# Moving the routing of a mixture-of-depths kernel: gate scores from V, comparisons on GpSimd, half stores on SP

## The chip, the cores and the metric

The kernel runs on one core of one Trainium2 chip. The metric is the device time of one execution in microseconds (us), lower is better; it is given as the median of the runs. "Span" is the time from the first to the last instruction in the profiled execution. The engines are called PE (TensorE, matmul), PEld (its weight loads), DVE or VectorE, ACT or ScalarE, POOL or GpSimd, and SP (SyncE, here a queue for DMAs).

## The reference

Two layers follow each other. The first is attention in chunks of 32 tokens: each chunk sees 16 tokens to its left, 8 to its right and 8 memory tokens of its head. The second is a mixture of depths: of the 768 tokens of a batch, the 128 with the highest gate score pass through a two-layer expert, and the result, times the sigmoid of the score, is added to the token.

```python
# attention: q, k, v are (4, 8, 768, 64); mem_k, mem_v are (4, 8, 8, 64)
for c in range(24):
    k_full = concat(mem_k, k[:, :, max(0, 32*c - 16) : min(768, 32*c + 40)])
    v_full = concat(mem_v, v[...same tokens...])
    a = softmax(q_c @ k_full.T / 8)
    out[:, :, 32*c : 32*c + 32] = a @ v_full
# mixture of depths: x is (4, 768, 512), the heads side by side
scores = x @ w_gate
for b in range(4):
    top = the 128 tokens with the largest scores[b]
    h = max(x[b, top] @ w1, 0)              # 512 -> 1024
    out[b, top] += sigmoid(scores[b, top])[:, None] * (h @ w2)
```

## The kernel before

**Pairs.** The work is cut into 16 pairs of heads (`n`), four to a batch. The main loop over `n` is written so that three pairs are in work at once. In iteration `n` stand, in this order: scores of pair n+1, first half (`scores`, PE matmuls, then three exponentials on ACT, L271); transposes of q for pair n+2 (`tr_q`); values of pair n, first half (`values`, L292); transposes of k for pair n+2 (`tr_k`); scores of n+1, second half; V of n+1 turned back (`back_v`, L250 and L251); values of n, second half; transposes of v for n+2 (`tr_v`). `values` multiplies the exponentials with 64 columns of V and a column of ones, so that column 64 of the result is the sum of the softmax; VectorE takes its reciprocal (L295) and writes x (L296). The 8 memory columns of k and v are copied into place on GpSimd (`mem_cols`, L224): those of kw(n+2) after VectorE's copy (L232), those of vw(n+3) earlier in the iteration.

**Routing.** For a finished batch the kernel runs these steps, each named `m_...`:

- `m_dot`: six multiply-and-accumulate instructions on VectorE (L335), the gate scores `scr`
- `m_row`: PE transposes the scores so that each partition sees all 768 of them, ACT copies them to `brow`
- `m_gate_exp`, `m_gate`: the sigmoid, an exponential on ACT and four small operations on VectorE (L361 to L365)
- `m_cmp`: six comparisons 128x768 of the row with each token's score (L373)
- `m_count`: 36 matmuls with a column of ones count them (L383), six per comparison
- `m_mask`, `m_slot`, `m_sel`: the chosen tokens, their places, and one-hot columns `sel`
- `m_fetch`: token numbers `idx` by six matmuls (`m_aux`, L438), then an indirect DMA on GpSimd's queue fetches the 128 rows from the stored output (L412)
- `m_rows`, `m_ffn1` (two halves, L453), `m_ffn2` (L462): the expert; then `y` on ACT and an indirect DMA that adds it to the output (L466)

**Order.** The order on each engine is the order of the program text. `moe_steps` gives each step of batch b a place, counted in eighths of a pair from the start of batch b+1; `hook(i)` in the loop emits what is due. Batches 0 and 1 have their comparisons at places 18, 19, 22, 23, 24 and 27 and their counts at 30 and 31; batch 2 has a denser list. Weights and later q, k and v are loaded by DMAs of GpSimd's queue at the end of some iterations (`load_w` in pairs 0, 2, 4 and 6, `load_unit` in pairs 1, 3, 5 and 7).

**The last batch.** Batch 3 has no later loop to hide in. Its dots over the first two pairs stand in iteration 15; after the loop come the store of x, the dots over the last two pairs, and the remaining steps by hand, with the expert of batch 2 among them. It doesn't fetch its rows: `m_gather` (L428) picks them by matmuls with `sel` from a half-precision copy `x16`. `fill` is a matmul with zeros that computes nothing.

**Buffers.** The PSUM pools `pxx` (values), `pvv`, `ptt` and `pmm` (routing) have one buffer each, `pss` has two. Batch 3 takes `pss` for its routing.

Of the kernel before, what the change touches and what calls it, by code (L numbers as in the profile page):

```python
# [17 lines left out]
def _dap(x, offset, dims):  # L18
    return bass.AP(tensor=x.tensor, offset=offset, ap=[list(d) for d in dims])
# [7 lines left out]
def kernel(  # L27
# [13 lines left out]
    nc = tc.nc  # L41
# [11 lines left out]
    NPR = B * NP  # L53
    SLOTS = 4

    cst = ctx.enter_context(tc.tile_pool(name="cst", bufs=1))
# [93 lines left out]
    for i in range(SLOTS):  # L150
        vcs.append(cst.tile([128, NG, 2, 66], F16, tag=f"vc{i}", name=f"vc{i}"))
        kws.append(cst.tile([128, NG, 128], F16, tag=f"kw{i}", name=f"kw{i}"))
        vws.append(cst.tile([128, NG, 128], F16, tag=f"vw{i}", name=f"vw{i}"))
        nc.vector.tensor_copy(out=vcs[i][:, :, :, 64], in_=ones8[:, :].unsqueeze(2).to_broadcast([128, NG, 2]))
# [19 lines left out]
    onec = cst.tile([128, 1], F16, tag="onec")  # L174
    zero6 = cst.tile([128, NB], F16, tag="zero6")
    auxs = [cst.tile([128, NB, 3], F16, tag=f"aux{i}", name=f"aux{i}") for i in range(2)]
    w1_sb = cst.tile([128, 4, F], F16, tag="w1")
    w2_sb = cst.tile([128, 8, Dm], F16, tag="w2")

    def late_constants():  # L180
        nc.vector.tensor_copy(out=ident, in_=ident16)
        nc.vector.memset(ones6, 1.0)
        nc.vector.memset(onec, 1.0)
        nc.vector.memset(zero6, 0.0)
        nc.gpsimd.iota(iota1, pattern=[[1, cap]], base=1, channel_multiplier=0, allow_small_or_imprecise_dtypes=True)
        nc.gpsimd.memset(ltri, 1.0)
        nc.gpsimd.affine_select(out=ltri, in_=ltri, pattern=[[1, 128]], compare_op=ALU.is_gt, fill=0.0,
                                base=0, channel_multiplier=-1)
        for a in auxs:
            nc.gpsimd.iota(a[0:96, :, 0], pattern=[[96, NB]], base=0, channel_multiplier=1,  # L190
                           allow_small_or_imprecise_dtypes=True)
            nc.gpsimd.iota(a[96:128, :, 0], pattern=[[32, NB]], base=576, channel_multiplier=1,
                           allow_small_or_imprecise_dtypes=True)

    def load_w(i):
# [49 lines left out]
    def back_v(n):  # L245
# [5 lines left out]
        nc.vector.tensor_copy(out=vcs[n % SLOTS][:, :, :, 0:64], in_=p_v)  # L251

    GROUPS = ((0, 1, 2, 6), (3, 4, 5, 7))
    ess = {}
# [22 lines left out]
    def values(n, half, fills=0):  # L277
# [8 lines left out]
        fill_into(p_w, fills)  # L286
        p_x = p_w[:, 0:390].rearrange("p (i h c) -> p i h c", i=3, h=2)
        for r0, r1, gis in ((0, 96, (0, 1, 2)), (96, 128, (3, 3, 3))):
            for i, gi in enumerate(gis):
                q0, q1 = (0, 96) if gi < 3 else (32 * i, 32 * i + 32)  # L290
                for h in range(2):
                    nc.tensor.matmul(out=p_x[r0:r1, i, h, :], lhsT=es[:, h, gi, q0:q1],  # L292
                                     rhs=vc[:, GROUPS[half][gi], h, 0:65], start=True, stop=True)
        rd = att.tile([128, 3, 2, 1], FP, tag="rd", name="rd")
        nc.vector.reciprocal(out=rd, in_=p_x[:, :, :, 64:65])  # L295
        nc.vector.tensor_tensor(  # L296
            out=xs[b].rearrange("p g (n h d) -> p n g h d", n=NP, d=D)[:, pr, 3 * half:3 * half + 3],
            in0=p_x[:, :, :, 0:64], in1=rd.to_broadcast([128, 3, 2, D]), op=ALU.mult)

# [14 lines left out]

    def m_store(b):
        x = xs[b]

        eng = nc.gpsimd if b == LAST else nc.sync
        eng.dma_start(out=_dap(out, b * S * Dm, [[Dm, 96], [96 * Dm, NB], [1, Dm]]), in_=x[0:96, :, :])
        eng.dma_start(out=_dap(out, (b * S + 576) * Dm, [[Dm, 32], [32 * Dm, NB], [1, Dm]]), in_=x[96:128, :, :])  # L320

# [6 lines left out]

    def m_dot(b, bls, pr0=0, pr1=NP, dst=None):
        m, x = mods[b], xs[b]  # L330
        dst = m.scr if dst is None else dst
        for bl in bls:
            c0, c1 = 2 * D * pr0, 2 * D * pr1
            junk = mod.tile([128, Dm], FP, tag="junk", name="junk")
            nc.vector.scalar_tensor_tensor(out=junk[:, c0:c1], in0=x[:, bl, c0:c1], scalar=1.0, in1=wgb[:, c0:c1],  # L335
                                           op0=ALU.mult, op1=ALU.mult, accum_out=dst[:, bl:bl + 1])

# [3 lines left out]

    def m_row(b, lo, hi, eng=None):
        m = mods[b]
        p_b = m_bank(b, None)
        for bl in range(lo, hi):
            nc.tensor.transpose(out=p_b[:, 0, 128 * (bl - lo):128 * (bl - lo) + 128],
                                in_=m.scr[:, bl:bl + 1].to_broadcast([128, 128]), identity=ident)
        o, i = m.brow[:, 128 * lo:128 * hi], p_b[:, 0, 0:128 * (hi - lo)]
        if eng == "dve":
            nc.vector.tensor_copy(out=o, in_=i)  # L350
        else:
            nc.scalar.copy(out=o, in_=i)

# [12 lines left out]

    def m_cmp(b, bls):

        m = mods[b]
        if 0 in bls:  # L370
            m.gr = mod.tile([128, NB, S], F16, tag="gr", name="gr")
        for bl in bls:
            nc.vector.tensor_scalar(out=m.gr[:, bl, :], in0=m.brow, scalar1=m.scr[:, bl:bl + 1], scalar2=None,  # L373
                                    op0=ALU.is_lt)

# [47 lines left out]
    def m_gather(b):  # L423
        m = mods[b]
        p_e = m_bank(b, None)
        for dch in range(4):
            for bl in range(NB):
                nc.tensor.matmul(out=p_e[:, 0, 128 * dch:128 * dch + 128],  # L428
                                 lhsT=m.x16[:, bl, 128 * dch:128 * dch + 128],
                                 rhs=m.sel[:, bl, :], start=(bl == 0), stop=(bl == NB - 1))  # L430
        m.xeT = mod.tile([128, 4, 128], F16, tag="xeT", name="xeT")
        nc.scalar.copy(out=m.xeT.rearrange("p c t -> p (c t)"), in_=p_e[:, 0, :])

# [23 lines left out]

    def m_ffn2(b):
        m = mods[b]
        p_y = m_bank(b, None)  # L460
        for fch in range(8):
            nc.tensor.matmul(out=p_y[:, 0, :], lhsT=m.hT[:, fch, :], rhs=w2_sb[:, fch, :],  # L462
                             start=(fch == 0), stop=(fch == 7))
        y = mod.tile([128, Dm], FP, tag="y", name="y")
        nc.scalar.activation(out=y, in_=p_y[:, 0, :], func=AF.Copy, scale=m.gate[:, 0:1])  # L465
        nc.gpsimd.indirect_dma_start(out=outf[0:(b + 1) * S, :], out_offset=bass.IndirectOffsetOnAxis(ap=m.idx[:, :1], axis=0),  # L466
                                     in_=y[:, :], in_offset=None, compute_op=ALU.add)

    def moe_steps(b):
# [3 lines left out]
        def at(i, f, *a):  # L473
            st.setdefault(i, []).append(lambda: f(b, *a))
# [6 lines left out]
        if b == LAST - 1:  # L481
            p = dict(dots=(0, 1, 3, 4, 6, 7), row0=9, row1=11, gate=12, cmps=(13, 14, 15, 17, 18, 19),
                     counts=(21, 21, 21, 22, 22, 22), mask=22, slot=24, sel=24, fetch=24)
        for i in range(NB):
# [5 lines left out]
        for i in range(NB):  # L490
            at(p["cmps"][i], m_cmp, (i,))
        for i in range(NB):
# [18 lines left out]
    def hook(i):  # L511
        for f in places.get(i, ()):
            f()
# [22 lines left out]
    late_constants()  # L536
    scrA = mod.tile([128, NB], FP, tag="scrA", name="scrA")
    scrB = mod.tile([128, NB], FP, tag="scrB", name="scrB")
    for n in range(NPR):
        b, pr = divmod(n, NP)  # L540
# [4 lines left out]
        if n == 1:  # L545
            nc.sync.dma_start(out=wgb, in_=_dap(moe_w_gate, 0, [[0, 128], [1, Dm]]))
        if n == NPR - 2:
            m_alloc(LAST)
        scores(n + 1, 0)
        hook(i)  # L550
        if n == NPR - 1:
            m_dot(LAST, range(NB), 0, 2, scrA)
        if 3 <= n + 3 < NPR:
            mem_cols(vws[(n + 3) % SLOTS], memvT, n + 3)
        tr_q(n + 2)
        hook(i + 1)
        values(n, 0, nf)
        hook(i + 2)
# [5 lines left out]
        hook(i + 4)  # L564
        back_v(n + 1)
        hook(i + 5)
        values(n, 1, 1)
        hook(i + 6)
# [8 lines left out]

    b = LAST
    m_store(b)
    m_dot(b, range(NB), 2, 4, scrB)  # L580
    nc.vector.tensor_tensor(out=mods[b].scr, in0=scrA, in1=scrB, op=ALU.add)
    fill(8)
    m_rows(b - 1)
    m_row(b, 0, 4)
    m_gate_exp(b)
    m_row(b, 4, 6, "dve")
    m_ffn1(b - 1, 0)
    m_ffn1(b - 1, 1)
    m_cmp(b, range(NB))
    m_ffn2(b - 1)  # L590
    m_x16(b, 0, 6, 2, 4)
    m_count(b, range(NB))
    m_mask(b)
    m_slot(b)
    fill(3)
    m_sel(b)
# [41 lines left out]
```

## Time and profile before

| What | Value |
|---|---|
| Median of 3 runs | 141.28 us |
| Lowest and highest | 140.58 and 144.77 us |
| Profiled execution, its own time | 139.08 us |
| Its span | 137.4 us |
| Busy: PE, PEld | 111.7 us (81%), 83.0 us (60%) |
| Busy: DVE, ACT, POOL | 87.5 us (64%), 80.0 us (58%), 50.5 us (37%) |
| Mean granted clock of TensorE | 0.936 |
| Comparisons L373 on VectorE | 24, mean 0.62 us |
| Dots L335 on VectorE | 30, mean 0.58 us |

The profile tells of one execution. A line of a timeline has the start, the time taken, the engine, the line of the kernel, the operation, what it writes and reads with shape and type, a count where several were merged, and in brackets how long the engine had been idle and what ended that. The windows view has one row for each stretch of time: busy time of PE, PEld, DVE, ACT and POOL with the number of instructions, then the clock that TensorE was granted, the mean busy share of the DMA engines and the GB/s.

### The profile page before, as it was taken

To read this page: it belongs to the slowest core of one execution; us is meant where nothing else is said; L and a number is where in the kernel's file an instruction comes from. 1 tells how busy PE (TensorE), PEld (TensorE's weight loads), DVE (VectorE), ACT (ScalarE), POOL (GpSimd) and SP (SyncE) were. 2 spreads that over 40 slices of the span, in tenths; PEclk is the share of its full clock that TensorE was granted. 3 is DMA by queue.
4 is the path that set the end of the run, shared out by engine and by line. 5 is a ranking of instruction groups with operands and counts; after the bars stand their busy time and mean duration, and the time that the engine had idled before them with its cause. 6 is when DMAs were issued, how large, how long until landed. Compare 5 with 4: busy or idle time off the path is not lost.

```text
span 137.4 us, 4727 instructions
## 1 busy us (share of the span) xinstructions
PE 111.7 (81%) x2024; PEld 83.0 (60%) x2024; DVE 87.5 (64%) x280; ACT 80.0 (58%) x159; POOL 50.5 (37%) x84
## 2 busy tenths in 40 slices
PE   6997688977998978989997999897797897888500
PEld 2355376866777756867885858685656555458100
DVE  3444556574799399889738955997954896651000
ACT  4047958779779859565676947858748005153300
POOL 6996364352683634914200226121004140040130
PEclk9999999999999999995599999999999559999995
DMA  2999999999999999999991002973001439606050
GB/s 63 173 146 184 203 206 206 205 212 206 205 248 287 278 208 206 205 235 290 286 185 23 0 7 19 268 252 43 0 5 12 67 38 260 203 0 81 0 70 6
DMA packets 15397, 19.90 MB, mean 145 GB/s; under 512 B 848, under 2 KB 11536, under 8 KB 15376
## 3 DMA queue, kind: packets, MB, share of 16 engines
q0 software_dynamic: 12832, 14.62, 63.4%
q1 hardware_dynamic: 2544, 4.98, 11.0%
q8 instruction: 16, 0.26, 0.7%
q14 instruction: 5, 0.04, 0.1%
HBM read 24.25 MB, written 7.34 MB: 230 GB/s over the span
## 4 chain that ended last, share of the span: by engine, by line
PE 31%; DVE 15%; ACT 14%; issue 14%; DMA 14%; POOL 6%; POOLq 1%
ACT es L271 7%; DMA q<-in_q_dram 7%; PE p_w L292 7%; PE p_t L210 5%; PE p_v L250 4%; DMA xe<-out_dram,idx 3%; DMA out_dram<-y,idx 3%; DVE junk L335 3%; DVE x L296 3%; ACT qT L219 3%; PE p_w L116 3%; PE p_m L462 3%; PE p_m L453 2%; DVE gr L373 2%; PE p_m L383 2%
## 5 line engine op out<-in xcount | busy, mean ns | idle before, releaser
L271 ACT ACTIVATE es<-p_s,maskb 128x256 f16<-128x256 f32 x96 | 38.8, 485 | 3.2 <-PE p_s L266 3.1
L292 PEld LDWEIGHTS <-es 128*32 128x32 f16 (+1 forms) x384 | 22.1, 116 | 4.4 <-issue 0.7
L292 PE MATMUL p_w<-vc,es 128*32 128x65 f16 (+1 forms) x384 | 24.4, 208 | 0.0
L242 ACT COPY vw<-p_t 128x960 f16<-128x960 f16 x16 | 15.4, 962 | 14.5 <-PE p_t L210 14.5
L224 POOL COPY kw<-memkT 128x64 f16<-128x64 f16 x12 | 8.0, 666 | 36.4 <-DVE kw L232 36.4
L296 DVE TENSOR_TENSOR x<-p_w,rd 128x384 f32<-128x384 f32 x32 | 17.8, 558 | 1.1
L219 ACT COPY qT<-p_q 128x768 f16<-128x768 f16 x16 | 13.0, 813 | 7.4 <-PE p_q L210 7.4
L335 DVE SCALAR_TENSOR_TENSOR junk<-x,wgb 128x512 f32<-128x512 f32 (+1 forms) x30 | 16.2, 582 | 0.0
L466 POOL DMA_INDIRECT out_dram<-y,idx x4 | 6.5, 1635 | 24.7 <-ACT y L465 23.4
L295 DVE RECIPROCAL rd<-p_w 128x6 f32<-128x6 f32 x32 | 6.1, 191 | 12.5 <-PE p_w L292 12.1
L373 DVE TENSOR_SCALAR gr<-brow,scr 128x768 f16<-128x768 f32 x24 | 14.0, 623 | 0.1
L116 PE MATMUL p_f<-zeros 128*128 128x512 f16 x36 | 12.8, 496 | 1.3 <-DVE zeros L110 1.3
L250 PE MATMUL p_v<-ident,vw 128*128 128x128 f16 x128 | 10.2, 225 | 4.3 <-ACT qT L219 4.3
L251 DVE COPY vc<-p_v 128x1024 f16<-128x1024 f16 x16 | 11.0, 687 | 4.3 <-PE p_v L250 4.1
L232 DVE COPY kw<-p_t 128x1024 f16<-128x1024 f16 x16 | 10.9, 683 | 3.5 <-PE p_t L210 3.4
L266 PE MATMUL p_s<-qT,kw 64*128 64x96 f16 x256 | 11.3, 209 | 0.3 <-POOL kw L224 0.3
L250 PEld LDWEIGHTS <-vw 128*128 128x128 f16 x128 | 8.1, 100 | 5.6 <-issue 4.1
L116 PEld LDWEIGHTS <-zeros 128*128 128x128 f16 x60 | 5.9, 110 | 8.9 <-issue 4.6
L210 PE MATMUL p_q<-ident,q 96*64 96x96 f16 x256 | 8.8, 213 | 2.6 <-DMA q<-in_q_dram 2.5
L116 PE MATMUL p_w<-zeros 128*128 128x512 f16 x24 | 9.8, 410 | 1.0 <-DVE x L296 1.0
L210 PEld LDWEIGHTS <-q 96*64 96x64 f16 x256 | 6.7, 113 | 4.5 <-DMA q<-in_q_dram 2.7
L453 PEld LDWEIGHTS <-w_sb 128*128 128x128 f16 x128 | 7.6, 97 | 2.5 <-issue 1.6
(112 smaller groups left out, 165.0 us busy)
## 6 DMA issues: line engine op xcount, KB each, us to landing
out_dram<-x SPq DMA_DIRECT2D x3, 1152.0 KB, 11.5
k<-in_k_dram POOLq DMA_DIRECT2D x7, 384.0 KB, 13.2
q<-in_q_dram POOLq DMA_DIRECT2D x7, 384.0 KB, 13.7
v<-in_v_dram POOLq DMA_DIRECT2D x7, 384.0 KB, 14.6
w_sb<-in_moe_w_dram POOLq DMA_DIRECT2D x8, 256.0 KB, 13.4
out_dram<-x SPq DMA_DIRECT2D x3, 384.0 KB, 13.2
out_dram<-x POOLq DMA_DIRECT2D x1, 1152.0 KB, 6.8
k<-in_k_dram POOLq DMA_DIRECT2D x2, 192.0 KB, 4.8
```

Of the source, the lines that this page charges most:

```text
L116: nc.tensor.matmul(out=ap, lhsT=zeros[:, 0:128], rhs=zeros, start=True, stop=True)
L210: nc.tensor.transpose(out=dst[64 * h:64 * h + 64, j, :], in_=src[n][:, h, 64 * j:64 * j + 64], identity=ident16[0:96, 0:96])
L219: nc.scalar.copy(out=qT, in_=p_q.rearrange("p j t -> p t j"))
L242: nc.scalar.copy(out=vw.rearrange("p g (j t) -> p g j t", t=16)[:, :, :, 0:15], in_=_sap(p_t, 0, [[12, NG], [100, 8], [1, 15]]))
L250: nc.tensor.transpose(out=p_v[:, g, :, :], in_=vws[n % SLOTS][:, g, :], identity=ident16)
L251: nc.vector.tensor_copy(out=vcs[n % SLOTS][:, :, :, 0:64], in_=p_v)
L266: nc.tensor.matmul(out=p_s[:, h, 96 * gi:96 * gi + 96], lhsT=kw[o:o + 64, g, :], rhs=qf[o:o + 64, 96 * g:96 * g + 96], start=True, stop=True)
L271: nc.scalar.activation(out=es[:, :, :, 32 * c:32 * c + 32], in_=pv[:, :, :, 32 * c:32 * c + 32], func=AF.Exp, bias=maskb[:, c:c + 1], scal ...
L292: nc.tensor.matmul(out=p_x[r0:r1, i, h, :], lhsT=es[:, h, gi, q0:q1], rhs=vc[:, GROUPS[half][gi], h, 0:65], start=True, stop=True)
L296: nc.vector.tensor_tensor(out=xs[b].rearrange("p g (n h d) -> p n g h d", n=NP, d=D)[:, pr, 3 * half:3 * half + 3], in0=p_x[:, :, :, 0:64] ...
L335: nc.vector.scalar_tensor_tensor(out=junk[:, c0:c1], in0=x[:, bl, c0:c1], scalar=1.0, in1=wgb[:, c0:c1], op0=ALU.mult, op1=ALU.mult, accum ...
L373: nc.vector.tensor_scalar(out=m.gr[:, bl, :], in0=m.brow, scalar1=m.scr[:, bl:bl + 1], scalar2=None, op0=ALU.is_lt)
```

## The change

Four things are changed.

1. For pairs 14 and 15 (`WGN` is 14) V gets two more columns per head: V times the gate weights of that head, as a half-precision value and its remainder (`gate_columns` once, `gate_v` for each of the two pairs). `values` then yields the gate score's share in columns 65 and 66; `score` scales it by the reciprocal and adds it up. `values` returns the write of x and the score as two functions, so that the caller places them. The dots over the first two pairs of batch 3 move from iteration 15 into iteration 14.
2. `m_cmp` runs on GpSimd unless an engine is given. That holds for all comparisons of batches 0 and 1 and for the first four of batch 2. The last two of batch 2 and all of batch 3 stay on VectorE.
3. The last store goes out in two halves on SP (`m_store` with `lo` and `hi`), each after its half of x.
4. Batch 2 gets earlier places, so that its fetch is issued in iteration 14; the loop ends with iteration 14, and pair 15 is written out after it, with steps of batch 3 and the expert of batch 2 in turns. `m_ffn2` can be done in two halves. `m_gather` now goes over the token blocks outside and the four column blocks inside, after a matmul with zeros that opens the bank. The fills after the loop are gone.

```diff
-        vcs.append(cst.tile([128, NG, 2, 66], F16, tag=f"vc{i}", name=f"vc{i}"))
+        vcs.append(cst.tile([128, NG, 2, 68], F16, tag=f"vc{i}", name=f"vc{i}"))
...
+    def gate_columns():
+
+        nc.vector.memset(wgd, 0.0)
+        for h in range(2):
+            r = slice(64 * h, 64 * h + 64)
+            nc.vector.tensor_copy(out=wgd[r, :, h, 0], in_=wgT[r, :])
+            nc.vector.tensor_tensor(out=wgd[r, :, h, 1], in0=wgT[r, :], in1=wgd[r, :, h, 0], op=ALU.subtract)
...
+    def gate_v(n, p_g):
+
+        vc = vcs[n % SLOTS]
+        for g in range(NG):
+            nc.tensor.matmul(out=p_g[:, 4 * g:4 * g + 4], lhsT=vws[n % SLOTS][:, g, :],
+                             rhs=wgd[:, n - WGN, :, :].rearrange("p h c -> p (h c)"), start=True, stop=True)
+        gv = att.tile([128, NG, 2], FP, tag="gv", name="gv")
+        nc.vector.reduce_sum(out=gv, in_=p_g[:, 0:4 * NG].rearrange("p (g h c) -> p g h c", h=2, c=2),
+                             axis=mybir.AxisListType.X)
+        nc.vector.tensor_copy(out=vc[:, :, :, 65], in_=gv)
+        nc.vector.tensor_tensor(out=vc[:, :, :, 66], in0=gv, in1=vc[:, :, :, 65], op=ALU.subtract)
...
+        def score():
+
+            t = parts[n - WGN][half]
+            nc.vector.tensor_tensor(out=t[:, :, 0:4].rearrange("p i (h c) -> p i h c", c=2), in0=p_x[:, :, :, 65:67],
+                                    in1=rd.to_broadcast([128, 3, 2, 2]), op=ALU.mult)
+            o = mods[b].scr[:, 3 * half:3 * half + 3] if n == NPR - 1 else parts[1][half][:, :, 4]
+            nc.vector.reduce_sum(out=o, in_=t, axis=mybir.AxisListType.X)
...
-            nc.vector.tensor_scalar(out=m.gr[:, bl, :], in0=m.brow, scalar1=m.scr[:, bl:bl + 1], scalar2=None,
-                                    op0=ALU.is_lt)
+            (eng or nc.gpsimd).tensor_scalar(out=m.gr[:, bl, c0:c1], in0=m.brow[:, c0:c1],
+                                             scalar1=m.scr[:, bl:bl + 1], scalar2=None, op0=ALU.is_lt)
...
-            p = dict(dots=(0, 1, 3, 4, 6, 7), row0=9, row1=11, gate=12, cmps=(13, 14, 15, 17, 18, 19),
-                     counts=(21, 21, 21, 22, 22, 22), mask=22, slot=24, sel=24, fetch=24)
+            p = dict(dots=(0, 1, 2, 3, 4, 5), row0=7, row1=9, gate=11, cmps=(10, 10, 10, 10, 11, 13),
+                     counts=(16,) * NB, mask=16, slot=19, sel=20, fetch=22)
...
-            at(p["cmps"][i], m_cmp, (i,))
+            at(p["cmps"][i], m_cmp, (i,), nc.vector if b == LAST - 1 and i > 3 else None)
...
-    for n in range(NPR):
+    for n in range(NPR - 1):
...
+            nc.sync.dma_start(out=wgT, in_=_dap(moe_w_gate, 2 * D * (WGN % NP), [[1, 128], [2 * D, 2]]))
+        if n == 4:
+            gate_columns()
...
-        if n == NPR - 1:
-            m_dot(LAST, range(NB), 0, 2, scrA)
...
-        values(n, 0, nf)
+        vA = values(n, 0, nf)
+        vA[0]()
+        if n == NPR - 2:
+            m_dot(LAST, (0, 1, 2))
+            vA[1]()
...
+        if n == NPR - 2:
+            gate_v(n + 1, p_t.bitcast(FP).rearrange("p j t -> p (j t)")[:, 0:4 * NG])
+            m_dot(LAST, (3, 4, 5))
...
-    b = LAST
-    m_store(b)
-    m_dot(b, range(NB), 2, 4, scrB)
-    nc.vector.tensor_tensor(out=mods[b].scr, in0=scrA, in1=scrB, op=ALU.add)
-    fill(8)
+    b, n = LAST, NPR - 1
+    A, Bh = range(3), range(3, 6)
+    vA = values(n, 0)
+    vA[1]()
+    vB = values(n, 1)
+    m_row(b, 0, 3, pxx.tile([128, 512], FP, tag="px", name="p_r"))
+    vB[1]()
+    vA[0]()
+    m_store(b, 0, 3)
+    m_row(b, 3, 6, pvv.tile([128, 512], FP, tag="pv", name="p_r"))
+    m_gate_exp(b)
     m_rows(b - 1)
-    m_row(b, 0, 4)
-    m_gate_exp(b)
-    m_row(b, 4, 6, "dve")
+    m_x16(b, 0, 3, 2, 4)
+    m_cmp(b, A, nc.vector, 0, S // 2)
     m_ffn1(b - 1, 0)
+    m_cmp(b, A, nc.vector, S // 2, S)
     m_ffn1(b - 1, 1)
-    m_cmp(b, range(NB))
-    m_ffn2(b - 1)
-    m_x16(b, 0, 6, 2, 4)
-    m_count(b, range(NB))
+    m_cmp(b, Bh, nc.vector)
+    vB[0]()
+    m_x16(b, 3, 6, 2, 4)
+    m_store(b, 3, 6)
+    m_count(b, A)
+    m_ffn2(b - 1, 0, 4)
+    m_count(b, Bh)
     m_mask(b)
     m_slot(b)
-    fill(3)
+    m_ffn2(b - 1, 4, 8)
     m_sel(b)
     m_gate(b)
     m_gather(b)
```

## The prediction

> **What bounds the kernel now.** I read the 40 slices first, then the time of each pair of heads (from one reciprocal of a pair's second half, L295, to the next), then the timeline around the routing of each batch, and last the tail.
>
> No engine bounds the span (PE 81%, DVE 64% busy), so each stage has its own limit. In the windows view (columns PE, PEld, DVE, ACT, POOL busy, clock, DMA share, GB/s) pairs 6, 9, 12 and 14 read:
>
> ```profile
> 44.66:51.24 6.58, 5.32 (x124) 4.17 (x121) 4.28 (x14) 4.65 (x11) 3.05 (x6) 1.00 1.19 245
> ...
> 62.75:69.71 6.96, 6.96 (x106) 5.74 (x108) 5.41 (x14) 4.54 (x9) 2.70 (x4) 0.59 1.15 276
> ...
> 83.67:91.30 7.63, 6.90 (x168) 5.58 (x168) 6.74 (x26) 4.52 (x10) 1.99 (x3) 1.00 0.81 210
> ...
> 97.06:105.28 8.22, 7.46 (x132) 5.71 (x127) 4.84 (x12) 5.92 (x12) 1.44 (x1) 1.00 0.01 3
> ```
>
> A pair without routing takes 4.7 us. Pair 6 waits in order on gate and comparisons, pair 9 runs at a 0.59 clock, pair 12 is nearly full of VectorE work, pair 14 carries the experts of batch 1 on PE.
>
> GpSimd looks free (37%), but its queue holds things that PE needs at once. The timeline around pairs 6 and 7:
>
> ```profile
> 50.26 0.78 POOL L224 COPY kw<-memkT 128x64 f16<-128x64 f16 x1 [3.53 <-DVE kw L232]
> 50.82 1.43 POOL L200 DMA_DIRECT2D w_sb<-in_moe_w_dram  x2
> 52.22 0.71 POOL L224 COPY vw<-memvT 128x64 f16<-128x64 f16 x1
> 55.23 0.79 POOL L224 COPY kw<-memkT 128x64 f16<-128x64 f16 x1 [2.29 <-DVE kw L232]
> ...
> 56.52 0.60 PE L383 MATMUL p_m<-onec,gr 128*128 128x1 f16 x18
> ...
> 57.05 0.34 PE L266 MATMUL p_s<-qT,kw 64*128 64x96 f16 x8
> ```
>
> The memory columns of kw are written there 1.8 us before scores reads them, and PE counts the comparisons (L383) just before the next scores. The tail:
>
> ```profile
> 108.23 0.16 DVE L441 TENSOR_SCALAR idx<-p_m 128x1 int32<-128x1 f32 x1 [0.28 <-PE p_m L438]
> 109.31 1.04 POOL L412 DMA_INDIRECT xe<-out_dram,idx  x1 [3.85 <-DVE junk L335]
> 115.75 3.26 DVE L373 TENSOR_SCALAR gr<-brow,scr 128x768 f16<-128x768 f32 x6
> 118.50 1.89 PE L462 MATMUL p_m<-w_sb,hT 128*128 128x512 f16 x8 [0.69 <-ACT hT L455]
> 120.25 1.04 PE L383 MATMUL p_l<-onec,gr 128*128 128x1 f16 x36
> 122.58 1.97 PE L428 MATMUL p_l<-sel,x 128*128 128x128 f16 x24
> 130.04 1.57 POOL L466 DMA_INDIRECT out_dram<-y,idx  x1 [6.97 <-ACT y L465]
> ```
>
> Around the end of attention stand 12 half dots and an add on VectorE (to 114.2), then rows, six comparisons to 119.0, then counts that still wait behind ffn2 of batch 2 on PE. From the last scatter to the end of the span it is 7.3 us in both kernels.
>
> **What the skill says.** The GPSIMD Engine Reference, "4.1 Engine selection", calls one-input elementwise work on GpSimd roughly line-rate, and its section 3.1 gives 1.03 to 1.8 cycles an element at 1.2 GHz. An estimate from that page for 768 elements is 0.66 to 1.15 us, without overhead. The trace has no long GpSimd operation: 64-element copies take 0.45 us, a 128-element select 0.29.
>
> SBUF — State Buffer, "Who interferes with whom": VectorE and GpSimd share one port pair as an exclusive lock, taken by two-port copies and tensor_scalars and by two SBUF inputs. The trace agrees: the kw copy at 43.59 took 0.85 beside a dot, 0.45 alone; a dot at 64.06 took 0.78 instead of 0.68 beside a vw copy.
>
> TensorE: Matmul & The Clock Gate, "Part 1: The HAM clock gate": a window with little PE work halves the clock. Here it is halved at 61.24 and at 105.61, 6.8 us each time.
>
> **Part by part.** The sum is against the profiled execution (139.08 us, span 137.4). Call one GpSimd comparison c. Below: 0.8 us (0.66 plus a small operation's overhead). Above: 1.5, by that page's 2.03 cycles an element for a compare that isn't unrolled (section 7). I take 1.1, the rate of the 128-element select carried to 768.
>
> (1) *Gate columns, pair 4*: five small VectorE operations of about 0.18 us. VectorE is full from 37.4 to 44.2 (3.36 of 3.41 us a window), with slack before: +0.3 (0 to 0.9). The two-column load on SP stands ahead of nothing urgent.
>
> (2) *Comparisons of batch 0 on GpSimd, pairs 6 and 7.* Six of 0.61 us leave VectorE, which helps little: the counts need all six. GpSimd's order becomes: comparison, kw(8), three comparisons, two weight loads (1.43), comparison, vw (0.5), kw(9) (0.5), comparison. The first can start at 47.5, when brow is there. Gate's four operations on VectorE (from 47.56) want the shared pair and can be blocked behind it. With kw(8) done between 50.2 and 50.8, the sixth ends at 50.2 + 2.4 + 5c or later: 56.6 at 0.8, 58.1 at 1.1, over 60 at 1.5. PE had its second counts at 56.52, and scores stands behind them. +1.7 (0.3 to 3.9).
>
> (3) *Batch 1, pairs 10 and 11.* The same lock at gate: the chain of waits there runs gate, reciprocal (73.46), x, values, so a block goes to the end: +0.5 (0 to 1.0). VectorE's relief is hidden, since PE has ffn1 and ffn2 of batch 0 there. The sixth comparison is queued behind the scatter of batch 0, which waits for y until 83.06 and ends at 84.73. It then ends near 85.9, against counts at 84.59: +1.1 (0.9 to 1.6).
>
> (4) *Batch 2 earlier, pairs 12 to 14.* All six dots now precede reciprocal (12, 1): two dots (1.38) more in a pair that is 6.74 of 7.63 full. The one-buffer p_w then delays values(13, 0), and the second half of brow, behind es and qT on ACT, comes near 95.7. Four comparisons on GpSimd (4c = 4.4) then stand ahead of kw(15), which scores(15, 0) needs at 98.45; gate and two comparisons on VectorE contend with them. In pair 14 VectorE gets six half dots (2.1), two gate_v (0.55 each), two scores (0.4 each), slot and sel (1.3), against 3.4 us idle today. Added up in order from reciprocal (13, 1), 97.7 at best, idx comes at 109.1 to 110.9 instead of 108.23. I take +1.3 (0.9 to 2.7). PE's eight gate matmuls (0.5) lie inside that.
>
> (5) *The tail, counted from idx.* Before: idx 108.23 to ffn1 of batch 3 at 125.28, 17.05 us. After: fetch issued at +0.4 and landed 4.0 later (at most 4.1 before, 4.8 for batch 1); rows and xeT 1.05 (to 5.45); ffn1 half 1.05, hT 0.65, half 1.05 (8.2); count A 0.55; half of ffn2 at 8.9 after hT, 0.95 (9.85); count B 0.5; mask and incl 0.45 (10.85); slot 0.2; second half of ffn2 0.95 (12.0); a 512-column zero matmul 0.25; 24 gather matmuls at 0.066 as in ffn1, 1.6 (13.9); xeT 0.7 (14.6). That is 2.45 less: −2.5 (−3.5 if the fetch lands in 3). The removed dots, add, fills and half of the comparisons' wait would give more; in their place the fetch is late, because dots no longer fill its flight. VectorE's own chain, with the two x writes, has its last comparison at +5.8, before PE's counts. The half stores on SP (an estimate of 3.5 us each: half of the 7 us that the DMA engines are busy after the store of 84.5) are over before the last scatter; nothing waits for them.
>
> (6) *The clock.* Without fill(8), PE has almost nothing from the values to the rows, some 4 to 5 us, so the half clock falls on ffn1 or later: two halves of ffn1 0.65 more each, counts and half of ffn2 0.9 to 1.4 more. +0.9 (0 to 2.7). The one at 105.61 covered mainly fills and dots, so nothing comes back.
>
> Sum: 0.3 + 1.7 + 0.5 + 1.1 + 1.3 − 2.5 + 0.9 = +3.3, or 142.4 us where this execution had 139.1. The median shown is 141.28, 2.2 above it (clock windows fall differently from run to run: 140.58 to 144.77), so 144.6.
>
> **Rivals.**
>
> *Even.* c is 0.8 and the gate gets the pair first: (2) 0.3, (3) 0.9, (4) 0.9, (1) 0.2, tail −2.5, clock 0.9: +0.7, so 142.0. For it: kw copies block a dot by only 0.1 us, so the lock is held shortly. Against: the load order in pair 6 and the scatter remain.
>
> *Faster: the tail decides.* One mechanism: PE stays at full clock and the fetch lands in 3 us, so ffn1 of batch 3 starts 3.5 us sooner after idx, while the half clock that pair 9 had (6.96 us, against 5 for pair 7) is missed since the windows fall elsewhere: about −2 more. With +2.3 in the loop, −3.2: 138.1. It decides once the loop's additions are under 0.7 us or that clock window goes. For it: the only window that halved pair 9 (57.8 to 61.2) was no emptier of PE work than others. Against: the new waits of PE lie right in front of it.
>
> *Still slower: the lock.* Gate, cast and both VectorE comparisons of batch 2 each wait a whole GpSimd comparison, c 1.3 or more: (2) 2.9, (4) 2.7: 147. It is within my slower case.
>
> **How the numbers follow.** A measurement of this kernel can tell about 2% from no change. Forecast with the lock, slower: 0.52. Even: 0.28. Faster: 0.20. The range leaves out half of the fast case and the worst of the lock: 138.0 to 148.5; the likeliest case's own is 144.1 to 148.5.
>
> **What would show it.** Right: GpSimd comparisons near 1.1 us; PE idle ahead of the second counts in pairs 7 and 11 and ahead of scores in pair 14; gate operations on VectorE longer than 0.2 us; PE idle before the rows of batch 2 and a half clock over ffn1. Wrong: comparisons at or under 0.8 us, no pair longer than before, or idx of batch 2 before 108.

## The result and the profile after

The changed kernel takes 165.44 us (median of 4 runs, 164.71 to 166.20) against 141.95 us for the kernel before (4 runs): 1.169 times as long, interval 1.157 to 1.182. Ratios and their intervals leave out executions more than 1.5% above the fastest of their kernel, so that a ratio need not be the quotient of the medians beside it. The prediction was 144.6 us in a range of 138.0 to 148.5. Its direction held; its size did not. In the profiled execution (164.71 us, span 163.0) the span is 25.6 us longer than before, and the mean granted clock fell from 0.936 to 0.781.

First the time from pair to pair, taken as before from one reciprocal (now L319) of a pair's second half to the next:

| Pair | 6 | 7 | 8 | 9 | 10 | 11 | 12 | 13 | 14 | 15 | last reciprocal to last scatter |
|---|---|---|---|---|---|---|---|---|---|---|---|
| before | 6.58 | 4.97 | 6.54 | 6.97 | 6.61 | 7.35 | 7.62 | 5.77 | 8.21 | 5.87 | 18.89 |
| after | 5.73 | 4.59 | 15.54 | 7.77 | 5.83 | 8.42 | 13.47 | 8.66 | 18.01 | 1.73 | 21.55 |

Three pairs carry most of it: 8 (+9.0), 12 (+5.9) and 14 (+9.8). Pair 13 (+2.9), pair 11 (+1.1) and the tail (+2.7) add to that, and pair 15 gives 4.1 back. Pairs 6, 7 and 10, from which VectorE lost its comparisons, did become 0.4 to 0.9 us shorter.

The windows view (PE, PEld, DVE, ACT, POOL busy, clock, DMA share, GB/s), first pair 8 of the kernel before:

```profile
56.21:62.75 6.54, 5.93 (x127) 4.68 (x125) 5.57 (x23) 3.96 (x8) 2.67 (x5) 0.92 1.20 234
```

and then pairs 6, 8, 9, 12 and 14 of the changed kernel:

```profile
44.41:50.14 5.73, 4.68 (x108) 3.63 (x104) 3.50 (x11) 4.23 (x10) 4.71 (x7) 1.00 1.18 252
54.74:70.28 15.54, 8.94 (x146) 7.00 (x146) 5.67 (x21) 4.06 (x8) 11.06 (x13) 0.58 1.18 246
70.28:78.05 7.77, 7.77 (x106) 6.33 (x108) 5.42 (x14) 4.55 (x9) 2.84 (x4) 0.51 0.36 58
92.30:105.77 13.47, 9.76 (x159) 7.66 (x159) 7.95 (x28) 4.33 (x10) 5.89 (x8) 0.60 0.55 138
114.43:132.44 18.01, 14.22 (x167) 10.25 (x164) 7.09 (x36) 7.10 (x12) 6.37 (x4) 0.53 0.09 10
```

In pair 8 PE is idle for 6.6 of 15.5 us while GpSimd is busy for 11, and what PE does, it does at 0.58 of its clock. Pair 9 is full of PE work at half clock. The page's costliest groups, and the waits of PE, name the cause (columns: total, times, and in the groups mean ns of one; in the waits the longest):

```profile
L408 POOL TENSOR_SCALAR gr<-brow,scr 128x768 f16<-128x768 f32 x16 | 36.1, 2265 | 8.0 <-ACT gt L392 5.2
```

```profile
PE p_m L418 <- POOL gr L408: 10.0, 4, 3.4
...
PE p_s L289 <- POOL kw L235: 2.1, 1, 2.1
...
PE p_g L268 <- DVE vc L262: 1.4, 1, 1.4
```

A comparison takes 2.2 us on GpSimd (median 2.200, shortest 2.190), where it took 0.61 on VectorE. The sixteen of them take 36 us of GpSimd's queue. The timeline around pairs 7 and 8 shows what stands behind them:

```profile
49.97 6.55 POOL L408 TENSOR_SCALAR gr<-brow,scr 128x768 f16<-128x768 f32 x3
...
56.47 1.49 POOL L211 DMA_DIRECT2D w_sb<-in_moe_w_dram  x2
...
57.99 2.21 POOL L408 TENSOR_SCALAR gr<-brow,scr 128x768 f16<-128x768 f32 x1
60.15 0.46 POOL L235 COPY vw<-memvT 128x64 f16<-128x64 f16 x1
60.26 0.32 PE L418 MATMUL p_m<-onec,gr 128*128 128x1 f16 x6 [3.38 <-POOL gr L408]
60.38 0.49 POOL L235 COPY kw<-memkT 128x64 f16<-128x64 f16 x1
60.65 2.19 POOL L408 TENSOR_SCALAR gr<-brow,scr 128x768 f16<-128x768 f32 x1
...
62.90 0.32 PE L418 MATMUL p_m<-onec,gr 128*128 128x1 f16 x6 [2.32 <-POOL gr L408]
63.15 0.50 PE L289 MATMUL p_s<-qT,kw 64*128 64x96 f16 x8
```

PE reaches the counts of the fourth comparison at about 55.7, and the last six counts run at 62.90. The next scores (L289) stand behind them in PE's order, so ACT and VectorE starve too. PE is granted the half clock from 57.4 to 77.9; before it was 6.8 us there.

The same in pairs 13 and 14, with the comparisons of batch 2:

```profile
109.55 9.21 POOL L408 TENSOR_SCALAR gr<-brow,scr 128x768 f16<-128x768 f32 x4 [2.78 <-ACT brow L387]
...
114.04 0.34 PE L268 MATMUL p_g<-wgd,vw 128*128 128x4 f16 x8 [1.42 <-DVE vc L262]
114.24 0.38 PE L454 MATMUL p_e<-ident,xe 128*128 128x128 f16 x4
...
118.71 0.44 POOL L235 COPY kw<-memkT 128x64 f16<-128x64 f16 x1
119.21 0.50 PE L289 MATMUL p_s<-qT,kw 64*128 64x96 f16 x8 [2.11 <-POOL kw L235]
...
128.63 0.16 PE L431 MATMUL p_m<-incl,ltri 128*128 128x1 f16 x1 [0.78 <-ACT y L503]
```

kw(15) waits behind four comparisons until 118.71 and scores with it. The gate matmuls of pair 14 (L268) wait for vc, and the rows of the expert of batch 1 (L454) come right after them. The slot of batch 2 (L431) waits for y of batch 1, since both use the one buffer of `pmm`.

And the tail:

```profile
133.44 0.16 DVE L476 TENSOR_SCALAR idx<-p_m 128x1 int32<-128x1 f32 x1
...
134.35 1.01 POOL L447 DMA_INDIRECT xe<-out_dram,idx  x1 [3.85 <-DVE rd L319]
...
138.18 0.61 PE L454 MATMUL p_e<-ident,xe 128*128 128x128 f16 x4 [2.28 <-DMA xe<-out_dram,idx]
...
139.46 1.86 PE L488 MATMUL p_m<-xeT,w_sb 128*128 128x128 f16 x16 [0.67 <-ACT xeT L456]
...
150.95 1.95 PE L488 MATMUL p_l<-xeT,w_sb 128*128 128x128 f16 x32 [0.99 <-DVE gate L478]
```

From idx to ffn1 of batch 3 it is 17.5 us, where it was 17.05 before and 14.6 in the prediction. The halves of ffn1 of batch 2 run at half clock (1.86 instead of 1.05).

### The profile page after: what moved, and what is told of

Read it like the earlier page. It is cut to its first block, busy times and chain, and to the rows that moved or that the text cites. A ratio compares the mean times of both kernels' runs of the same rounds, so it can differ in the third digit from the quotient of the medians.

```text
span 163.0 us, 4753 instructions
## 1 busy us (share of the span) xinstructions
PE 123.5 (76%) x2028; PEld 93.2 (57%) x2028; DVE 81.3 (50%) x272; ACT 81.0 (50%) x161; POOL 82.7 (51%) x98
## 5 line engine op out<-in xcount | busy, mean ns | idle before, releaser
L408 POOL TENSOR_SCALAR gr<-brow,scr 128x768 f16<-128x768 f32 x16 | 36.1, 2265 | 8.0 <-ACT gt L392 5.2
L316 PEld LDWEIGHTS <-es 128*32 128x32 f16 (+1 forms) x384 | 24.7, 127 | 5.2 <-issue 1.8
L316 PE MATMUL p_w<-vc,es 128*96 128x65 f16 (+3 forms) x384 | 27.3, 221 | 0.0
L253 ACT COPY vw<-p_t 128x960 f16<-128x960 f16 x16 | 15.4, 963 | 16.5 <-PE p_t L221 13.4
L322 DVE TENSOR_TENSOR x<-p_w,rd 128x384 f32<-128x384 f32 x32 | 17.8, 557 | 1.0
L319 DVE RECIPROCAL rd<-p_w 128x6 f32<-128x6 f32 x32 | 6.2, 192 | 20.1 <-PE p_w L316 19.7
L261 PE MATMUL p_v<-ident,vw 128*128 128x128 f16 x128 | 11.9, 247 | 4.8 <-ACT qT L230 4.8
L374 DVE SCALAR_TENSOR_TENSOR junk<-x,wgb 128x512 f32<-128x512 f32 (+1 forms) x24 | 14.3, 625 | 0.0
L289 PE MATMUL p_s<-qT,kw 64*128 64x96 f16 x256 | 12.6, 226 | 2.1 <-POOL kw L235 2.1
L261 PEld LDWEIGHTS <-vw 128*128 128x128 f16 x128 | 9.5, 111 | 6.4 <-issue 4.7
L488 PEld LDWEIGHTS <-w_sb 128*128 128x128 f16 x128 | 10.4, 121 | 3.5 <-issue 2.1
L418 PE MATMUL p_m<-onec,gr 128*128 128x1 f16 x108 | 4.0, 165 | 10.0 <-POOL gr L408 10.0
L289 PEld LDWEIGHTS <-kw 64*128 64x128 f16 x256 | 7.3, 103 | 7.2 <-issue 2.5
L418 PEld LDWEIGHTS <-gr 128*128 128x128 f16 x144 | 4.6, 101 | 11.8 <-POOL gr L408 10.4
## 6 DMA issues: line engine op xcount, KB each, us to landing
q<-in_q_dram POOLq DMA_DIRECT2D x7, 384.0 KB, 13.6
w_sb<-in_moe_w_dram POOLq DMA_DIRECT2D x8, 256.0 KB, 13.6
```

What stands on the lines that cost most here:

```text
L253: nc.scalar.copy(out=vw.rearrange("p g (j t) -> p g j t", t=16)[:, :, :, 0:15], in_=_sap(p_t, 0, [[12, NG], [100, 8], [1, 15]]))
L261: nc.tensor.transpose(out=p_v[:, g, :, :], in_=vws[n % SLOTS][:, g, :], identity=ident16)
L289: nc.tensor.matmul(out=p_s[:, h, 96 * gi:96 * gi + 96], lhsT=kw[o:o + 64, g, :], rhs=qf[o:o + 64, 96 * g:96 * g + 96], start=True, stop=True)
L322: nc.vector.tensor_tensor(out=xs[b].rearrange("p g (n h d) -> p n g h d", n=NP, d=D)[:, pr, 3 * half:3 * half + 3], in0=p_x[:, :, :, 0:64] ...
L408: (eng or nc.gpsimd).tensor_scalar(out=m.gr[:, bl, c0:c1], in0=m.brow[:, c0:c1], scalar1=m.scr[:, bl:bl + 1], scalar2=None, op0=ALU.is_lt)
L488: nc.tensor.matmul(out=p_h[:, 0, 128 * fi:128 * fi + 128], lhsT=w1_sb[:, dch, f0:f0 + 128], rhs=m.xeT[:, dch, :], start=(dch == 0), stop=( ...
```

## The experiments

Two theories stood at the start. *Queue:* GpSimd's comparisons hold up kw and PE's counts, and everything else follows from that. *Order:* the new places of batch 2 and the gate columns, with PE's fixed order, cost most of it, whoever compares.

**All comparisons back on VectorE.**

```diff
-            (eng or nc.gpsimd).tensor_scalar(out=m.gr[:, bl, c0:c1], in0=m.brow[:, c0:c1],
+            (eng or nc.vector).tensor_scalar(out=m.gr[:, bl, c0:c1], in0=m.brow[:, c0:c1],
```

> The changed kernel with one edit: every comparison on VectorE again, at the same places. Queue theory (comparisons of 2.2 us on GpSimd hold up the counts and the memory columns behind them, and nearly all of the loss follows from that): the pairs 8, 12 and 14 fall back to at most 7, 8.5 and 9.5 us, the time to 138 to 145 us, within 3% of the kernel before. Rival, order theory (batch 2's earlier places and the new tail cost much by themselves): over 148 us, with pair 14 still over 11 us.

Measured: 149.66 us (148.05 to 153.17), 1.067 times the kernel before (1.050 to 1.083). Pair 8 is back at 6.73 us, but pairs 12 to 14 take 31.45 together where the kernel before took 21.60. This is what the order theory had forecast for this run. So GpSimd is the larger part, and not the only one. What is left is again a queue, now on VectorE. The timeline of this run:

```profile
98.17 2.19 DVE L408 TENSOR_SCALAR gr<-brow,scr 128x768 f16<-128x768 f32 x4
...
102.16 0.68 DVE L262 COPY vc<-p_v 128x1024 f16<-128x1024 f16 x1
...
102.89 0.34 PE L268 MATMUL p_g<-wgd,vw 128*128 128x4 f16 x8 [3.42 <-DVE vc L262]
```

The comparisons of batch 2 stand ahead of the copy to vc, PE's gate matmuls wait for the bank that this copy empties, and the rows of the expert of batch 1 run only at 103.09, 9.3 us after their fetch was issued (93.79). In the kernel before they ran 4.8 us after it:

```profile
91.58 1.01 POOL L412 DMA_INDIRECT xe<-out_dram,idx  x1 [2.71 <-DVE rd L295]
...
96.40 0.40 PE L419 MATMUL p_e<-ident,xe 128*128 128x128 f16 x4
```

**GpSimd's comparisons alone:** the kernel before, with the comparisons of batches 0 and 1 on GpSimd.

```diff
-            nc.vector.tensor_scalar(out=m.gr[:, bl, :], in0=m.brow, scalar1=m.scr[:, bl:bl + 1], scalar2=None,
+            eng = nc.gpsimd if b < LAST - 1 else nc.vector
+            eng.tensor_scalar(out=m.gr[:, bl, :], in0=m.brow, scalar1=m.scr[:, bl:bl + 1], scalar2=None,
```

> The kernel before with one edit: the comparisons of batches 0 and 1 on GpSimd, all else as before. Queue theory: pair 8 at 15 us and pair 12 at 12 us as in the changed kernel, so 12 to 16 us slower, 153 to 158 us. Order theory: at most 6 us slower, since most of the loss would need the other edits.

Measured: 157.13 us (156.58 to 158.05), 1.122 times before (1.109 to 1.135), which is 14.8 us more than the 142.35 of the kernel before beside it. Pair 8 takes 15.56 us and pair 12 takes 12.41, where the changed kernel has 15.54 and 13.47. The two ratios multiplied, 1.122 and 1.067, give 1.197, a little more than the 1.169 of the whole change: two causes that nearly add up. This run moves the comparisons of batches 0 and 1 alone, and costs 14.8 us between medians; putting all of them back, the four of batch 2 too, won 15.8 (165.44 − 149.66). So the four of batch 2, though kw(15) waits for them, seem to add little; no run tests them alone.

**What a GpSimd operation costs.** Eighteen operations on GpSimd follow the last scatter of the kernel before; nothing uses their results, and the run's 169.1 us are longer only for them.

```diff
+    for _ in range(2):
+        nc.gpsimd.tensor_scalar(out=pa, in0=br, scalar1=sc[:, 0:1], scalar2=None, op0=ALU.is_lt)
+    for _ in range(2):
+        nc.gpsimd.tensor_scalar(out=pa[:, 0:384], in0=br[:, 0:384], scalar1=sc[:, 0:1], scalar2=None, op0=ALU.is_lt)
...
+    for _ in range(2):
+        nc.gpsimd.tensor_copy(out=pc, in_=br)
```

> The kernel before with eighteen GpSimd operations added after its last scatter is issued, two each: comparisons of 768, 384 and 96 columns, with 32-bit output, with half-precision input, against a constant, a multiplication in place of the comparison, and copies to half and to full precision; their outputs are used by nothing. If the 2.2 us are a rate (2.8 ns an element), 384 columns take 1.1 to 1.2 and 96 about 0.4 us, and the multiplication is as slow. If they are the cost of comparing, the multiplication and the copies take about 0.8 us. If they are contention with VectorE, which is idle here, 768 columns take 1.2 us or less.

Groups by line in this run (total us, mean ns of one):

```profile
L617 POOL TENSOR_SCALAR pa<-brow,scr 128x768 f16<-128x768 f32 x2 | 4.4, 2204 | 0.1
L623 POOL TENSOR_SCALAR pa<-pc,scr 128x768 f16<-128x768 f16 x2 | 4.4, 2201 | 0.2
L615 POOL TENSOR_SCALAR pb<-brow,scr 128x768 f32<-128x768 f32 x2 | 4.4, 2200 | 0.1
L619 POOL TENSOR_SCALAR pa<-brow 128x768 f16<-128x768 f32 x2 | 4.3, 2128 | 0.2
L611 POOL TENSOR_SCALAR pa<-brow,scr 128x384 f16<-128x384 f32 x2 | 2.5, 1240 | 0.2
...
L621 POOL CAST pc<-brow 128x768 f16<-128x768 f32 x2 | 1.6, 823 | 0.1
L613 POOL TENSOR_SCALAR pa<-brow,scr 128x96 f16<-128x96 f32 x2 | 1.0, 520 | 0.2
```

A multiplication (L617) takes as long as a comparison; so does one with half-precision input (L623), one with single-precision output (L615), and, almost, one with a constant (L619). (The comparison of 768 columns itself has a mean of 2.49 here, since the first of its two, 2.79 us, begins before the scatter ahead of it has ended; the second takes 2.19.) From 384 to 768 elements it is 0.96 us, from 96 to 384 it is 0.72: 2.5 ns an element both times, and 0.28 us besides. VectorE is idle here, so a shared port is not the reason. A cast of the same 768 elements takes 0.82 us.

**How much the clock adds.** In the changed kernel, matmuls with zeros on PE (4, 16 and 12) ahead of the counts of the last three comparisons of batches 0 and 1, where PE waits.

```diff
+            if b < LAST - 1 and bl >= 3:
+                fill((4, 16, 12)[bl - 3])
```

> The changed kernel with zero matmuls (4, 16 and 12 of 512 columns) put ahead of the fourth, fifth and sixth counts of batches 0 and 1, where TensorE sits idle for GpSimd; the waits stay. If the half clock that follows the waits carries much of the loss, the clock stays full in pairs 8, 9 and 12 and the time falls by 4 to 8 us, to 157 to 161. If the waits alone carry it, the time stays within 2 us of the changed kernel (165).

Measured: 165.36 us (163.37 to 170.23), no different from the changed kernel, at a mean clock of 0.865 instead of 0.781. In pairs 8 and 9 the half clock is gone and they take 14.05 and 5.29, 4.0 us less; but pairs 11 and 12 take 3.2 more, where the fills run from 89.5 to 97.0 and outlast a wait that was 3.4 us long. So the clock was worth about 4 us in batch 0. That is all of the half clock there, not what the change added: the kernel before has a half clock in the same pairs. For the whole kernel this run decides nothing.

**The places of batch 2 as before,** with all comparisons on VectorE.

```diff
-            p = dict(dots=(0, 1, 2, 3, 4, 5), row0=7, row1=9, gate=11, cmps=(10, 10, 10, 10, 11, 13),
-                     counts=(16,) * NB, mask=16, slot=19, sel=20, fetch=22)
+            p = dict(dots=(0, 1, 3, 4, 6, 7), row0=9, row1=11, gate=12, cmps=(13, 14, 15, 17, 18, 19),
+                     counts=(21, 21, 21, 22, 22, 22), mask=22, slot=24, sel=24, fetch=24)
...
     A, Bh = range(3), range(3, 6)
+    hook(8 * n)
```

> All comparisons on VectorE, and batch 2 at the places that it had before (its slot, sel and fetch then stand right after the loop, ahead of pair 15); gate columns, new tail and half stores stay. Places theory (the earlier list puts four comparisons ahead of kw(15) and of vc(14) on VectorE, so gate_v and behind it the rows and ffn1 of batch 1 come 6 us late): pairs 12 to 14 take 22 to 24 us together instead of 31.5, and the time falls from 149.7 to 142 to 145 us. Tail theory (the new tail is what costs): stays at 148 to 150.

Measured: 144.62 us (142.77 to 145.50), 1.031 times before (1.015 to 1.046): 5.0 us less than with the new places. In the trace pairs 12 and 13 are back at 7.62 and 5.77.

**Only the gate matmuls of pair 14 later,** behind the first half of ffn1 of batch 1, with the new places and all comparisons on VectorE.

```diff
-        if n == NPR - 3:
-            gate_v(n + 1, pvv.tile([128, 512], FP, tag="pv", name="p_g"))
         hook(i + 6)
         tr_v(n + 2)
         hook(i + 7)
+        if n == NPR - 3:
+            gate_v(n + 1, pvv.tile([128, 512], FP, tag="pv", name="p_g"))
```

> All comparisons on VectorE and the earlier places kept, but gate_v of pair 14 moved in iteration 13 from ahead of the rows of batch 1 to behind its ffn1. If gate_v's wait is what holds up the expert of batch 1, rows of batch 1 start within 1 us of the landing of their fetch and pairs 13 and 14 lose 3 to 5 us together: 145 to 147. If the four comparisons ahead of kw(15) do it by themselves, under 1.5 us is won: 148.5 to 150.

Measured: 145.14 us (144.70 to 146.70), 1.046 times before (1.033 to 1.059); pair 14 takes 10.43 instead of 13.43. By the ratios (1.067 and 1.046) one small group of matmuls in front of the expert was worth about 3 us, and the traces agree: pairs 12 to 15 take 30.23 together instead of 33.10, where the kernel before took 27.48. The medians, 4.5 us apart, also hold what the kernel before differed between the two occasions (142.35 and 141.21). Pairs 13 and 14 lose 2.9 together, a little under the 3 to 5 expected, and the rows still run about 3.5 us after their fetch has landed, not within 1 us. The move acts on pair 14 alone: pairs 12 and 13 stay at 8.84 and 9.30 (7.63 and 5.76 before), and only the old places bring them back. So the places of batch 2 cost something of their own, besides the wait of the gate matmuls.

**Fills in the tail.** The kernel with all comparisons on VectorE and the places of before, and twelve fills ahead of the rows of batch 2.

```diff
     m_gate_exp(b)
+    fill(12)
     m_rows(b - 1)
```

> As the kernel with batch 2's places of before, plus 12 zero matmuls of 512 columns in the tail between the rows of batch 3 and those of batch 2, where TensorE waits for the fetch. If the half clock in the tail costs 1.5 to 3 us, that much is won against the same kernel without them. If the wait for the fetch is all, the two are within 0.8 us, or this one is slower by what the fills overrun.

Measured: 142.69 us (140.67 to 147.30), 1.018 times before (1.000 to 1.036). Pairs 12, 13 and 14 take 7.62, 5.77 and 9.58, but pair 11 takes 11.31, of which more is said with the next run. The expert of batch 2 has its full clock (ffn1 1.05), yet from idx to ffn1 of batch 3 it is still 17.8 us: the fills took 4.35 us, partly at half clock themselves, and the rows ran at 118.56, 7.2 us after their fetch was issued.

**Two comparisons on GpSimd instead of six,** in the kernel before.

```diff
-            nc.vector.tensor_scalar(out=m.gr[:, bl, :], in0=m.brow, scalar1=m.scr[:, bl:bl + 1], scalar2=None,
+            eng = nc.gpsimd if b < LAST - 1 and bl < 2 else nc.vector
+            eng.tensor_scalar(out=m.gr[:, bl, :], in0=m.brow, scalar1=m.scr[:, bl:bl + 1], scalar2=None,
```

> The kernel before with the first two of six comparisons of batches 0 and 1 on GpSimd, the other four on VectorE. Queue theory: 2.2 us hurt only where something waits for them; the first ends at 49.4 before kw(8) is due, the second near 52.2 before the counts at 54.7, and VectorE is relieved in pairs 6 and 10, which fall from 6.6 to 5.8 us each: 1 to 2 us faster than before, 139 to 141.5. Cost theory (any comparison on GpSimd costs its difference of 1.6 us): 4 to 6 us slower.

Measured: 141.49 us (140.19 to 144.00), 1.012 times before (1.000 to 1.023): anything from no change to 2.3% slower, and not the 1 to 2 us faster that were expected. The cost theory (4 to 6 us slower) falls. Where the two comparisons stand they hold nothing up: pairs 6 and 10 take 5.81 and 5.45 (6.58 and 6.61 before). But pair 11 takes 11.19 instead of 7.35, partly at half clock. The loop now arrives at the expert of batch 0 sooner than its rows do:

```profile
74.27 0.40 PE L420 MATMUL p_e<-ident,xe 128*128 128x128 f16 x4 [1.69 <-DMA xe<-out_dram,idx]
```

That fetch was issued at 62.27, 12 us earlier, among the loads of later q, k and v. In the kernel before, the rows ran at 75.07 with no such wait. The long pair 11 is not the price of GpSimd: in the run with twelve fills, where VectorE does every comparison, it takes 11.31, with the same wait:

```profile
74.16 0.61 PE L454 MATMUL p_e<-ident,xe 128*128 128x128 f16 x4 [1.89 <-DMA xe<-out_dram,idx]
```

In both runs pair 9 escaped the half clock (5.27 and 5.25 us instead of 6.96), which brings the loop to these rows earlier.

**Fills where PE really waits.** Again all comparisons on VectorE and the places of before, now with eight fills ahead of mask and slot of batch 2, and four instead of twelve ahead of the rows.

```diff
     A, Bh = range(3), range(3, 6)
+    fill_into(pvv.tile([128, 512], FP, tag="pv", name="p_f"), 8)
     hook(8 * n)
...
     m_gate_exp(b)
+    fill(4)
     m_rows(b - 1)
```

> The kernel with all comparisons on VectorE and the places of before for batch 2, plus two fills on PE: eight matmuls with zeros ahead of mask and slot of batch 2 (PE waits 1.9 us there) and four ahead of the rows of batch 2 instead of twelve. Two theories of the missing gain of the tail. Clock: the order of the tail is worth what was predicted and only the half clock ate it; then the window that began at 110.8 goes, rows follow the fetch at about 114.6, the time from idx of batch 2 to ffn1 of batch 3 is 14.0 to 15.5 us and the median 138 to 140.5 us, at or a little under the kernel before. Order: the tail is bound by VectorE's comparisons and ACT's copies whatever the clock; then the time from idx to ffn1 stays at 16.5 to 18 us and the median at 141.5 to 144.

Measured: 140.00 us (136.73 to 144.97, 22 runs) against 141.87 (43 runs) for the kernel before; the ratio is 0.992 (0.988 to 0.997): 0.8% less, within the 2% that count as the same here. The tail of this run:

```profile
106.70 1.89 PE L117 MATMUL p_f<-zeros 128*128 128x512 f16 x8
...
110.60 0.16 DVE L476 TENSOR_SCALAR idx<-p_m 128x1 int32<-128x1 f32 x1 [0.27 <-PE p_m L473]
...
111.03 1.00 POOL L447 DMA_INDIRECT xe<-out_dram,idx  x1 [4.31 <-DVE gate L478]
...
114.32 0.40 PE L454 MATMUL p_e<-ident,xe 128*128 128x128 f16 x4 [0.33 <-DMA xe<-out_dram,idx]
...
115.39 1.05 PE L488 MATMUL p_m<-xeT,w_sb 128*128 128x128 f16 x16 [0.67 <-ACT xeT L456]
...
124.11 1.95 PE L488 MATMUL p_l<-xeT,w_sb 128*128 128x128 f16 x32 [0.60 <-ACT xeT L467]
```

From idx to ffn1 of batch 3 it is 13.5 us, 3.5 less than before, and no half clock lies between 70 us and 130 us. The same order without any fills (the run with the places of before, in an execution of 145.50 us) took 18.4 us there, at half clock from 109.8 to 130.6. The clock theory of the tail held; the order theory (16.5 to 18 us) fell.

**The same with two comparisons on GpSimd.**

```diff
-            (eng or nc.vector).tensor_scalar(out=m.gr[:, bl, c0:c1], in0=m.brow[:, c0:c1],
+            eng = nc.gpsimd if b < LAST - 1 and bl < 2 else nc.vector
+            eng.tensor_scalar(out=m.gr[:, bl, c0:c1], in0=m.brow[:, c0:c1],
```

> The same kernel with the first two of the six comparisons of batches 0 and 1 on GpSimd, at their places. If a GpSimd comparison of 2.2 us costs nothing where nobody waits for it, pairs 6 and 10 become 0.8 to 1.1 us shorter as in the run with two comparisons on GpSimd, and the whole is 0 to 1.5 us faster than the kernel without; if what VectorE gains is given back in the next pairs (pair 7 longer by 0.5, pair 11 by several us if its fetch or a half clock falls there), it is the same or up to 2 us slower.

Measured: 138.65 us (137.03 to 140.56, 22 runs), ratio 0.993 (0.989 to 0.997): by the ratios the same as without GpSimd, though the median is 1.35 us lower. Its trace is of an execution of 140.56 us, the longest of the 22. There pairs 6 and 10 gain (5.73 and 5.45), and pair 11 takes 10.27, with a wait of 0.8 us for its fetch, after a pair 9 of 5.29.

## Why the prediction was wrong

The failed step is the first one of the part-by-part: "Call one GpSimd comparison c ... Above: 1.5 ... I take 1.1". It is 2.2 us, twice the value and beyond the upper bound, and it went into three terms of the sum. It is not the whole miss: without any comparison on GpSimd the changed kernel is still 1.067 times the kernel before, and that part belongs to steps 4 and 6. The estimate came from the GPSIMD Engine Reference, "4.1 Engine selection", where one-input work is roughly line-rate. A cast fits the estimate drawn from it (0.82 us for 768 elements, estimated 0.66 to 1.15), a tensor_scalar does not: 2.5 ns an element is, as an estimate with that page's 1.2 GHz, about 3 cycles. Closer was a row that I had not used, the two-input addition of its section 3.1, 2048 elements in 4497 ns, 2.2 ns an element. My second source, the 128-element select of 0.29 us carried to 768, was another operation.

*Step 2* had the mechanism and the formula. "The sixth ends at 50.2 + 2.4 + 5c or later" gives 63.6 with the measured c, and it ended at 62.84. PE's counts then stand at 62.90 instead of 56.52: 6.4 us where the sum had +1.7. Pair 8 also began 1.5 us sooner than before (54.74 against 56.21). That leaves 1.1 of its +9.0, and the run with fills ahead of the counts, where the clock stays full, took 1.5 off pair 8.

*Step 3* named the right victim, the sixth comparison of batch 1, but the wrong reason. Not the scatter that waits for y delayed it: y was ready at 91.4, but five comparisons held GpSimd from 80.9 to 92.4, and two copies, the scatter and the sixth comparison came after them. PE waited 3.4 us for the sixth until 97.08. It was priced at +1.6 with the gate; in the run with these comparisons alone pairs 11 and 12 grew by 5.9.

*Step 4* was mis-sized twice. Its "four comparisons (4c = 4.4) ahead of kw(15)" took 9.2. And its PE side, "eight gate matmuls (0.5) lie inside that", counted their busy time and not what they wait for. They stand ahead of the expert's rows, and vc's copy is queued behind comparisons on VectorE (this is seen in the run with all comparisons there). Even without GpSimd, pairs 12 to 14 lengthened by 9.85 us, of which pair 15 gave back 4.2 (1.66 against 5.87), where the step had +1.3. Moving these matmuls alone brought about 3 us.

*Step 5* was right about the order and about 1 us too careful: 14.6 predicted, 13.5 measured with the clock full; 0.7 of that is the fetch, whose rows ran 3.7 us after idx and not at 4.4. In the changed kernel the gain is absent: the clock of step 6 took most of it, through halves of ffn1 at 1.86 and a half of ffn2 at 1.78, and the fetch, issued at +0.9 after idx and its rows at +4.7, took 0.3 us more. The step's "nothing waits for them", said of the half stores, is in doubt: where the first of them was issued within 0.9 us after the fetch, the rows came 3.8 to 5.7 us after the fetch (four runs, the changed kernel among them), and where the store came 1.9 us or more after it, the fetch landed in 3.2 to 3.3 us (six runs). No run moves the store alone, so this is not shown.

*Step 6*, the clock, was too small. (Its reading, "halved at 61.24 and at 105.61", names the starts of two stretches of the windows view; the half clock begins some 0.5 us later in both.) It was priced in the tail alone, at +0.9. In the loop, where it was not priced, the half clock took about 4 us in pairs 8 and 9. The kernel before already paid some of that: its pairs 8 and 9 take 13.50 us, and 11.65 in the run with twelve fills, where the clock is full there. So the change added about 2 us in these two pairs. TensorE: Matmul & The Clock Gate, "What's actually happening", has a window of about 3.4 us with PE idle halve the clock. The trace agrees in the length alone: the clock is half from 57.4 to 77.9, 20.5 us or about six such windows. Its start does not fit, since it comes 0.5 us into the long wait, after 3.4 us (53.99 to 57.40) in which PE was busy for 2.03. And it stays for 13.6 us (64.22 to 77.88) with hardly a gap in PE's work. What exactly starts and ends it is not settled here. The three waits of pair 8 (0.9, 3.4 and 2.3 us) go with it, and such a loss of PE's work must be charged the clock as well.

*Step 1* was right to be small: pair 4 took 4.77 instead of 4.67.

Of the rivals, *the lock* had the direction but not the cause. SBUF — State Buffer, "Who interferes with whom", says that the side that comes second blocks for the whole instruction. In the trace two of the four gate operations beside a 2.2-us comparison took 0.81 and 0.62 in batch 2 and one took 0.46 in batch 0, where the same operations take 0.16 to 0.21 with all comparisons on VectorE. So those that were held lose 0.3 to 0.65 us each and never 2.2; why so little is not settled. *Faster: the tail decides* was not this kernel's case, but its mechanism exists: freed of the two queues and of the half clock, the tail gives the only versions with an interval below that of no change (0.992 and 0.993).

Still open: what of the earlier places of batch 2 lengthens pairs 12 and 13; whether the half store slows the fetch; and whether an earlier fetch of batch 0 would turn the gain of two GpSimd comparisons into time.

## What to carry to other kernels

Before moving an operation to another engine, price it at that engine with its own opcode; here a cast's 0.82 us said nothing of a tensor_scalar's 2.2. If no row shows the operation, make the upper bound wide enough for a factor of two. Then write down what follows it in that engine's queue: here two comparisons cost too little to be told (1.012, 1.000 to 1.023), and six, with the copies and counts behind them, cost 15 us. In this kernel waits of several us on PE cost their length and went with a half clock; matmuls with zeros helped where they filled a gap that PE had anyway (eight in a wait of 1.9 us), and not where they outlasted it (twelve took 4.35 us).

## What the hardware showed that I had not expected

On GpSimd a tensor_scalar over 128 partitions took 0.28 us and 2.5 ns an element, whatever the operation (comparison, multiplication) and the types (half or single precision on either side), while a copy or cast of 768 elements took 0.82 us. VectorE does the same comparison in 0.61 us. A fetch of 128 rows landed in 3.2 to 3.3 us in tails where no store followed within 1.9 us, had its rows used after 3.8 to 5.7 where one followed within 0.9, and took up to 12 us while the loads of later pairs were under way. TensorE's clock stayed half for 13.6 us in which it was busy almost throughout.
